# Memory read of a segmented attention as two row-half products, its last step on GpSimd, and vector steps with one operand in PSUM

## The chip, the cores and the metric

The kernel runs on one core of a Trainium2 chip. The metric is the device time of one execution in microseconds (us). The engines are TensorE (PE, with its weight loads PEld), VectorE (DVE), ScalarE (ACT), GpSimd (POOL) and SyncE (SP), whose queue issues most DMAs.

## The reference, cut to what matters

The output is `x + attention(xn) + mlp(xn)`, where `xn` is the layer-normalised input of 2048 tokens by 512. The attention has 32 heads of 16 and goes over 4 segments of 512 tokens. In each segment it mixes a causal softmax with a read of a memory that the earlier segments filled:

```python
for s in range(N):
    qs, ks, vs = q[:, :, s], k[:, :, s], v[:, :, s]
    logits = jnp.einsum("bhqd,bhkd->bhqk", qs, ks) * scale + mask
    p = _softmax(logits, axis=-1)
    a_dot = jnp.einsum("bhqk,bhkd->bhqd", p, vs)
    pq = phi(qs)                       # t + 1 where t > 0, exp(t) elsewhere
    num = jnp.einsum("bhld,bhde->bhle", pq, M)
    den = jnp.einsum("bhld,bhd->bhl", pq, z)[..., None] + 1e-6
    a_mem = num / den
    o = g * a_mem + (1.0 - g) * a_dot  # g = sigmoid(beta), one per head
    outs.append(o)
    pk = phi(ks)
    M = M + jnp.einsum("bhld,bhle->bhde", pk, vs)
    z = z + jnp.einsum("bhld->bhd", pk)
```

The MLP is a second layer norm, 512 to 1792 with GELU, and back to 512. All is float32.

## The kernel before, in words

The work is cut into 16 units: 4 segments times 4 groups of 8 heads (`i = 4 * s + g`). For a unit, queries and keys stand with 8 heads x 16 = 128 rows on the partitions and the segment's 512 tokens as columns. Beside the units runs the MLP in 16 half jobs (`d_job` for the first product, `gelu`, `h_split` for splitting the result in two f16 parts, `e` steps for the second product). Float32 products are made of f16 halves where the weights allow (`split3`: three products for one).

The steps of a unit, by the names that the profile's lines belong to:

- `qk_proj` (L599): projection of queries or keys, 12 matmuls of 512 columns at L586, then on ScalarE the high f16 half (L614) and, where `phi` is wanted, the exponential (L618). `qk_low` (L624) makes the low half on VectorE and sends both to DRAM over the SP queue; `qk_rows` (L646) loads them back in another layout, with 48 rows for each of two row halves.
- `qk_phi` (L632, L634, L638): two VectorE instructions, the first from SBUF to SBUF.
- `m_job` (L740, L747): products of 48 rows in the two row halves of the array, whose row maxima VectorE takes. `m_row` (L753 to L758) and `max_rows` (L763) carry the maxima through DRAM into two more rows of the queries' operand.
- `s_job` (L782, L789): the logits again, now with the maxima subtracted, and their exponentials on ScalarE; `s_mask` (L803) on GpSimd; `pv` (L816) the product with the values in four column tiles, in f32; `o_norm` the division: part 0 a shuffle, part 1 logarithm and exponential on ScalarE (L657, L658), part 2 a newton step on VectorE (L662, L663), part 3 on GpSimd the multiplication (L847) and the addition of the memory read (L849), parts 4 and 5 the split in halves.
- the memory: `pk_nat` (L651) turns the keys, `kv` (L717) adds to the memory `mst` and `zst`. For segments 1 to 3, `z_cols` (L670, L673) spreads `mst` and `zst` over the heads on VectorE, `a_mem` (L681 to L689) makes the read with the tokens as rows (4 products with 136 columns in f32, then six VectorE instructions with a reciprocal), and `a_turn` (L696, L698) turns it back with 4 transposes and a copy by ScalarE into `ame`.
- `out_jobs` (L951, L953): the output projection of a segment, added to the accumulator that `store` sends out.

The weights are loaded, scaled by a power of two (`w_scale`, L414) that comes from a sum of squares (`w_trace`, L382 and L384) and split in halves in the first 60 to 100 us, among the first units' work.

The schedule is written out by hand. `streams()` lists chains of steps, each with its name, a letter. The string `ORDER` says from which chain the next step is taken, and every engine's queue gets its instructions in that order. `BANKS` says for every product in turn which of PSUM's eight banks it takes; `dense()` draws the next digit. `plan()` also sets where ScalarE's tables are changed.

Of the kernel before, what the change touches and what calls it, by code (L numbers as in the profile page):

```python
# [9 lines left out]
F32 = mybir.dt.float32  # L10
# [9 lines left out]
P = 128  # L20
# [39 lines left out]
def streams():  # L60
# [78 lines left out]
    "auhhwhhhlkhhkhhbth6xc6khldlhhie$hfhhhhkjhx6f78$hhahhv$rg7%%8%k8%h8bR8cs8mRde8i&ff9m9gj9n&!n&#y&z((CA)9*(CD+(+2"  # L139
    "BBDo)(X*+X,)-,*(()X!*3oXX,9,XXYFZFF0Py1F.zpF,-o!FR4F#.Z-0FB9,.14BR4QFZF041/XZA,X/01/-/.4F$=4/=p:4E4P24#F2;F:=="  # L140
    "44:4G4GFGX=GF<XHGFF3>4HaI>::IHI>IFGqGb3Xc?X2GH;GFyFFdzG@XHf>XF:EHYCX<X?DiQZ0IIA>;IB1I>GJG<3KGXCLBe:XGG;ZHD@MPX"
    "4HNFFIIHQIO0IFFG1Z4f4<GGX?0@41GHHqFZFy0FGY>F4a[1?4zXjAFHFZIIIIb4@0B4414Z[[FEcJ4KXXd4440[1eBXfGGGZ4LXXFMG440G]F"
    "1FH4fUN4ZP^H0X1YFFFyH4OFFIIIZiAIGzF044444GFGCF]GGX4_ETX1H]H4Q]HIIIDIGJGKBGZH4LPVX0BaXy1ZzG0GFMC4X1H4AZ4^FID0H_"
    "NOIITIFG4XGFUG4H4G1GFHBH4XFFIIIIFFJYFKURR4B4FLFMbFZNFRXOE0S4W4GcFGeX4144HGGGRF5HFIIHQIIdFFGSZG5FHFPyG0GGXzSFH1"
    "Z2VHASIIQIEI0GJGKLGXC13BX2DPfUXTGMGW444fNZV44H0HHjIIIOQIBFFG41a4bGGX4iHGGF3Y44H4HFFF4yFZ5FI01IIzBZAI0F1JZFX04X"
    "C4K1DZ404FjXX1B44X4EXX4YT4Z44LFG2cG4M44eGFiFd01X43H4FGGZN0HXXFF5IHIIOIGFGXXGGF2XWFG1FZfHf0XPVHFU4441Z01YZyE44H"
    "a3zIIIQIGGJ44UK4L4C4AGGMTG4D4N4WH4bPHHOIIIIGGGXB0BVXGGFyFF1HzHHBFIcIdAIZIRCFFFe01RDXFJKFFXZi0RLMXXFWTN41fR4fE4"
    "GZGGB4440XHOG1FGH4SHFFFIIYIQISGGa5FVZ4X4GG0UFXP4HH2FG1Z0FbyH4FzFIQIIAI1S5XSPBFZJ4X03KLCc1EZDM4GiGT5NOG4XBXGGj4"
    "H4W0HH4IQIII1GGF444FGG4VXGFFyHHHFFFIYIII24dZ4e440F13zFZ0FJ4XC4D1Z0XXFEfXK41BTABXL4Z4XM44041GGGPX44UGFFH44HNU4f"
    "4OFYZGF04WXV44XH1F2ZFIIIIFGFy53G0zFFXX1XGHZGG44FHC440TXXXIED1QYI2HZI0IGG41JKH4BZjj44GGGH34L4UBMX4HWNXX0OIIIIFF"  # L150
# [902 lines left out]
```

## Time and profile before

| | |
|---|---|
| median of 3 runs | 691.14 us (690.75 to 691.84) |
| span of the profiled execution, first to last instruction | 690.7 us |
| PE busy | 680.1 us, 98% |
| PEld busy | 394.6 us, 57% |
| DVE busy | 498.9 us, 72% |
| ACT busy | 471.4 us, 68% |
| POOL busy | 346.4 us, 50% |
| DMA | 55.83 MB, mean 81 GB/s |

The profiled execution's own time is its span; the timed runs are other executions of the same program, and their median lies 0.4 us above it. A matmul's length in the profile holds the time until its last column has left the array, so that neighbours overlap: what a matmul costs is the distance from its start to the next one's. A group row reads: line, engine, operation, output and inputs, shapes, count, then busy time and mean length in ns, then the idle time of the engine ahead of it and what ended it. A row of the timeline begins with start and length in us. A row for one line alone gives the least, median and greatest length in ns and the first and last start. A row by stretches gives the stretch and, for each engine, its busy time in it.

### The profile page before, as it was taken

Reading aid. Unit: us, or ns where it says so; the run is one execution under the profiler, and the core shown is the slowest. Engines: PE = TensorE matmul, PEld = TensorE weight load, DVE = VectorE, ACT = ScalarE, POOL = GpSimd, SP = SyncE. Lnnn points to the kernel's source line nnn. Section 1 sums busy time; section 2 is a strip of 40 time slices with the busy share of each in tenths; the row PEclk is TensorE's granted clock in tenths of the full one; section 3 lists DMA queues with packets and bytes.
Section 4 is the critical chain, followed back from the end, with each engine's and each line's share of the span. In section 5 each row is a group of like instructions: output and inputs, shape, how many; then the busy total and the mean of one; then the engine's idle time right before and its main releaser. Section 6 shows DMA issues by size and latency. Waiting matters only on the chain.

```text
span 690.7 us, 15732 instructions
## 1 busy us (share of the span) xinstructions
PE 680.1 (98%) x5787; PEld 394.6 (57%) x5787; DVE 498.9 (72%) x1613; ACT 471.4 (68%) x877; POOL 346.4 (50%) x574
## 2 busy tenths in 40 slices
PE   8999999999999999999999999999999999999997
PEld 6764565656644565665555555566565446565543
DVE  5789888986796669676695875878468565787622
ACT  4578898897765578578836838556956554777960
POOL 5576587663525444373545344534372425365652
PEclk9999999999999999999999999999999999999999
DMA  9788433203320342312222133231411222420101
GB/s 267 230 199 218 113 91 105 79 2 91 81 49 16 87 108 55 95 47 72 70 70 57 31 79 86 57 85 39 99 35 56 69 65 61 107 65 2 33 1 61
DMA packets 52889, 55.83 MB, mean 81 GB/s; under 512 B 4990, under 2 KB 41868, under 8 KB 52812
## 3 DMA queue, kind: packets, MB, share of 16 engines
q1 hardware_dynamic: 50508, 50.64, 26.8%
q0 software_dynamic: 2304, 4.20, 3.8%
q8 instruction: 45, 0.74, 0.5%
q14 instruction: 32, 0.26, 0.1%
HBM read 37.77 MB, written 17.05 MB: 79 GB/s over the span
## 4 chain that ended last, share of the span: by engine, by line
PE 87%; DVE 8%; DMA 2%; issue 1%; SPq 1%; POOL 1%; ACT 0%; DVEq 0%
PE dense L586 35%; PE dense L931 20%; PE dense L816 10%; PE dense L951 6%; PE dense L782 6%; PE dense L740 5%; DVE dense L747 4%; PE dense L681 2%; PE dense L696 1%; DVE mc L747 1%; PE dense L564 1%; DMA pt<-in_A_wv_dram 1%; PE dense L651 1%; DMA qst<-md 1%; PE dense L382 0%
## 5 line engine op out<-in xcount | busy, mean ns | idle before, releaser
L747 DVE CUSTOM_DVE_ANT_0 dense<-dense,mask 128x384 f32<-128x384 f32 (+3 forms) x512 | 234.0, 528 | 33.9 <-PE dense L740 33.6
L789 ACT ACTIVATE pt<-dense,qkcs 128x512 f32<-128x512 f32 (+1 forms) x384 | 204.2, 628 | 46.3 <-PE dense L782 46.2
L931 PE MATMUL dense<-w2s,hT 128*128 128x512 f16 x672 | 166.3, 380 | 0.2 <-DVE hT L884 0.2
L586 PE MATMUL dense<-xnT,w1s 128*128 128x256 f16 x1344 | 160.2, 273 | 0.3 <-DVE mc L747 0.3
L803 POOL TENSOR_SCALAR_AFFINE_SELECT pt<-pt 128x256 f32<-128x256 f32 x256 | 99.4, 422 | 108.2 <-ACT pt L789 107.8
L586 PEld LDWEIGHTS <-w1s 128*128 128x128 f16 x1344 | 129.6, 98 | 29.1 <-issue 6.2
L905 POOL TENSOR_TENSOR hT<-hh,hT 128x512 f16<-128x512 f32 x64 | 67.6, 1057 | 83.6 <-ACT hT L903 70.4
L931 PEld LDWEIGHTS <-hT 128*128 128x128 f16 x672 | 61.3, 98 | 68.6 <-issue 13.4
L816 PE MATMUL dense<-pt,vt 128*32 128x512 f32 (+3 forms) x1024 | 78.0, 436 | 0.0
L747 DVE DVE_READ_ACCUMULATOR2_ANT mc<- 128x1 f32 x512 | 74.2, 145 | 0.0
L884 DVE SCALAR_TENSOR_TENSOR hT<-dense,sc,cb 128x512 f32<-128x512 f32 x64 | 43.5, 680 | 33.8 <-PE dense L586 25.2
L847 POOL TENSOR_TENSOR nN<-nN,oT 128x512 f32<-128x512 f32 x16 | 20.9, 1308 | 73.9 <-DVE oT L663 73.9
L901 POOL TENSOR_SCALAR hh<-hT,sc 128x512 f32<-128x512 f32 x64 | 42.5, 664 | 24.1 <-ACT hT L891 15.5
L816 PEld LDWEIGHTS dense<-pt,vt 128*32 128x32 f32 x1024 | 31.1, 109 | 40.7 <-issue 29.4
L782 PE MATMUL dense<-qst,kst 50*128 50x384 f16 (+3 forms) x512 | 52.1, 299 | 1.8 <-DMA qst<-md 1.8
L740 PE MATMUL dense<-kst,qst 48*128 48x384 f16 (+3 forms) x512 | 52.2, 298 | 0.0
L891 ACT ACTIVATE hT<-hT,b1t 128x256 f32<-128x256 f32 x112 | 47.0, 496 | 5.0 <-DVE hT L884 4.6
L903 ACT ACTIVATE hT<-hh 128x512 f16<-128x512 f32 x64 | 37.3, 583 | 14.9 <-POOL hh L901 14.9
L951 PE MATMUL dense<-wos,oT 128*128 128x512 f16 (+2 forms) x204 | 44.0, 367 | 0.8 <-DVE acc L953 0.7
L586 PE MATMUL dense<-xnT,wks 128*128 128x512 f16 (+1 forms) x252 | 44.5, 329 | 0.2 <-DVE mc L747 0.2
L586 PE MATMUL dense<-xnT,wqs 128*128 128x512 f16 (+1 forms) x252 | 44.2, 329 | 0.1
L586 PE MATMUL dense<-wvs,xnT 128*128 128x512 f16 x192 | 43.9, 379 | 0.1
(227 smaller groups left out, 832.0 us busy)
## 6 DMA issues: line engine op xcount, KB each, us to landing
kst<-kd SPq DMA_DIRECT2D x32, 192.0 KB
qst<-qd SPq DMA_DIRECT2D x32, 192.0 KB
qd<-hl SPq DMA_DIRECT2D x36, 128.0 KB
kd<-hl SPq DMA_DIRECT2D x33, 128.0 KB
acc<-in_A_x_dram SPq DMA_DIRECT2D x16, 256.0 KB
acc<-in_B_b_dram POOLq DMA_DIRECT2D x16, 256.0 KB, 4.2
out_dram<-acc SPq DMA_DIRECT2D x15, 256.0 KB
xt<-in_A_x_dram SPq DMA_DIRECT2D x14, 256.0 KB
```

The costliest lines, as they stand in the source:

```text
L586: T.matmul(p, ws(k, a), xs(k, b), start=i == 0, stop=i == 3 * KT - 1)
L740: T.matmul(p[:, o:o + n], stk[i, 0][r, t, P * qb:P * qb + P], stk[i, 1][r, t, :n], start=True, stop=True)
L747: V.tensor_tensor_reduce(p[:, o:o + n], p[:, o:o + n], mask[:, 512 - n:], 1.0, -3e38, OP.add, OP.max, mc[i][:, 4 * b + t, qb:qb + 1])
L782: T.matmul(p[:, o:o + n], stk[i, 1][r, t, P * kb:P * kb + P], stk[i, 0][r, t, P * kb:], start=True, stop=True)
L789: A.activation(pt[i, 4 * b + t][:, OFF[kb]:OFF[kb] + n], p[:, c:c + n], AF.Exp, scale=qkcs[:, 1, i % NG:i % NG + 1])
L803: G.affine_select(v, v, pattern=[[0, 2], [1, P]], compare_op=OP.is_ge, fill=0.0, base=0, channel_multiplier=-1)
L816: T.matmul(p[32 * c:32 * c + 32, P * kb:], vt[s, kb][:, 4 * g + c, 16 * odd:16 * odd + 32], pt[i, 2 * c + odd][:, OFF[kb]:OFF[kb] + LEN[kb ...
L884: V.scalar_tensor_tensor(hz[:, f0:f + 1, :], p[:, :256 * n].rearrange("p (f c) -> p f c", f=n), col(CG + fh), cbt[hf].unsqueeze(1).to_broa ...
L891: A.activation(hz[:, f, :], hz[:, f, :], AF.Gelu_apprx_tanh, bias=b1t[:, fo:fo + 1])
L905: G.tensor_tensor(hT[:, z, 1, :], hht[j, c], hT[:, z, 0, :], op=OP.subtract)
L931: T.matmul(p, t[:, u, P * a:P * a + P], w2s[:, fo, v, :], start=fi == 0 and n == 0, stop=fi == FH - 1 and n == 2)
L951: T.matmul(p[:, c], o[:, u, P * b:P * b + P], wos[:, g, v, c], start=i == 0, stop=i == 3 * NG - 1)
```

## The change

- **phi.** `qk_proj` no longer makes the exponential. A new step `qk_floor` (`Tu`) has VectorE write `max(p * c, 0)` from PSUM into SBUF and ScalarE make the exponential from PSUM into the same PSUM bank. `qk_phi` is one VectorE instruction, `min(exp, 1) + floor`, with one operand in PSUM and one in SBUF.
- **memory read.** `z_cols` runs on GpSimd and writes 128 columns, which hold 64 of the memory with the gate's factor and 64 of the normaliser. `a_mem` has the tokens as columns: two f32 products, one with the upper and one with the lower 64 rows, each giving 64 rows of numerators and 64 of denominators by 512 columns. ScalarE takes the denominators' logarithm (two instructions of 64 rows) and one exponential of the negative. `a_share` (`Y`) has four VectorE instructions of 64 rows, each with one operand in PSUM. `a_step` (`Yg`) ends it with two GpSimd instructions. The turn by TensorE, its copy and the reciprocal are gone.
- **softmax division.** `o_norm` part 1 writes the exponential to a PSUM bank, and the newton step reads it there.
- **small things.** The addition to `zst` moves to GpSimd; `gates` and `qk_scale` have fewer small instructions.
- **order.** `ORDER` and `BANKS` are new as a whole: from the step `T` of unit 0 on, the steps stand in another order, the last steps too.

```diff
@@ streams @@
             put(n + "1", ("Tv", i, w))
             if not (s == 0, s == NSEG - 1)[w]:
+                put(n + "1", ("Tu", i, w))
                 put(n + "2", ("Tw", i, w))
...
-            put("mem2", ("Qt", i))
+            put("mem2", ("Y", i))
+            put("mem3", ("Yg", i))
@@ ORDER, BANKS: new strings @@
@@ qk_proj @@
-        e = None
-        if phi:
-            e = sb.tile([P, 512], F32, name=("phq", "phk")[which])
-            A.activation(e, p, AF.Exp, scale=qkcol(2, 1 - which, g))
-        prj[i, which] = p, hl, e
+        prj[i, which] = p, hl
...
+    def qk_floor(i, which):
+        g = i % NG
+        p = prj[i, which][0]
+        e = pqt[i, which] = sb.tile([P, 512], F32, name=("phq", "phk")[which])
+        c = qkcol(2, 1 - which, g)
+        V.tensor_scalar(e, p, c, 0.0, op0=OP.mult, op1=OP.max)
+        A.activation(p, p, AF.Exp, scale=c)
+
     def qk_phi(i, which):
...
-        V.tensor_scalar(e, e, 1.0, qkcol(3, 1 - which, g), op0=OP.min, op1=OP.mult)
         if which == 0:
-            V.scalar_tensor_tensor(e, p, 0.0, e, op0=OP.max, op1=OP.add)
+            V.scalar_tensor_tensor(e, p, 1.0, e, op0=OP.min, op1=OP.add)
@@ the memory read @@
     def z_cols(i):
-        g = i % NG
-        mx[i] = sm.tile([P, P + GH], F32, name="mx")
-        V.tensor_tensor(mx[i][:, :P] ...
-        V.tensor_scalar(mx[i][:, P:], half, zst[:, g:g + 1], None, op0=OP.mult)
+        s, g = divmod(i, NG)
+        if s == 1:
+            G.tensor_scalar(quadg[:, g], quad, bg[:, g, 3:4], 0.0, op0=OP.mult, op1=OP.add)
+        mx[i] = sm.tile([P, P], F32, name="mx")
+        G.tensor_tensor(mx[i][:, :64] ...
+        G.tensor_scalar(mx[i][:, 64:] ...
     def a_mem(i):
-        for t in range(4):
-            T.matmul(ps[t // 2][:, t % 2, :], pqt[i, 0][:, P * t:P * t + P], mx[i], start=True, stop=True)
-        (six VectorE instructions, L684 to L691)
-    def a_turn(i):
-        for t in range(4):
-            T.transpose(p[:, P * t:P * t + P], amt[i][:, P * t:P * t + P], ident)
-        ame[i] = sb.tile([P, 512], F32, name="ame")
-        A.activation(ame[i], p, AF.Copy)
+        q = pqt[i, 0]
+        mp[i] = [dense() for b in range(2)]
+        R = [slice(64 * b, 64 * b + 64) for b in range(2)]
+        for r, p in zip(R, mp[i]):
+            T.matmul(p, mx[i][r, :], q[r, :], start=True, stop=True)
+        for r, p in zip(R, mp[i]):
+            A.activation(q[r, :], p[64:, :], AF.Ln, bias=tiny[:64])
+        A.activation(q, q, AF.Exp, scale=-1.0)
+
+    def a_share(i):
+        q = pqt[i, 0]
+        t = ame[i] = sb.tile([P, 512], F32, name="ame", bufs=2)
+        R = [slice(64 * b, 64 * b + 64) for b in range(2)]
+        for r, p in zip(R, mp[i]):
+            V.tensor_tensor(t[r, :], p[:64, :], q[r, :], op=OP.mult)
+            V.scalar_tensor_tensor(q[r, :], p[64:, :], 1e-6, q[r, :], op0=OP.add, op1=OP.mult)
+
+    def a_step(i):
+        q, t = pqt[i, 0], ame[i]
+        G.tensor_scalar(q, q, -2.0, 0.0, op0=OP.add, op1=OP.add)
+        G.tensor_tensor(t, t, q, op=OP.mult)
@@ kv @@
-        V.tensor_tensor(zst[:, g:g + 1], zs[i], zst[:, g:g + 1], op=OP.add)
+        G.tensor_tensor(zst[:, g:g + 1], zs[i], zst[:, g:g + 1], op=OP.add)
@@ o_norm @@
         elif part == 1:
-            log_recip(nd[i][2], d)
+            rec[i] = dense()
+            A.activation(d, nd[i][2], AF.Ln)
+            A.activation(rec[i], d, AF.Exp, scale=-1.0)
         elif part == 2:
-            newton(nd[i][2], nd[i][2], d)
+            r = nd[i][2]
+            V.tensor_tensor(r, r, rec[i], op=OP.mult)
+            V.scalar_tensor_tensor(r, r, 2.0, rec[i], op0=OP.subtract, op1=OP.mult)
```

More of the change, by code (lines that the diff above doesn't have):

```diff
@@ L144 @@
[L144 to L148, printed above, removed]
@@ L399, in qk_scale @@
         h = h.unsqueeze(2).to_broadcast([P, 2, n])
-        f, s, c, t = (qksc[:, j, :, g0:g0 + n] for j in range(4))
+        f, s, c = (qksc[:, j, :, g0:g0 + n] for j in range(3))
         power(s, h, -1, 203)
```

121 lines of the change are left out of this document (52 added, 69 removed).

## The prediction

> **What bounds the kernel now.** I read the page first (engine shares, the chain that ended last), then the groups of instructions with shapes kept apart, then the timeline of TensorE where the changed products stand.
>
> ```profile
> span 690.7 us, 15732 instructions
> PE 680.1 (98%) x5787; PEld 394.6 (57%) x5787; DVE 498.9 (72%) x1613; ACT 471.4 (68%) x877; POOL 346.4 (50%) x574
> PEclk9999999999999999999999999999999999999999
> PE 87%; DVE 8%; DMA 2%; issue 1%; SPq 1%; POOL 1%; ACT 0%; DVEq 0%
> ```
>
> TensorE is busy for 98% of the span at full clock, and 87% of the chain that ended last is its work; no other engine is over 72%. The sum is therefore one of TensorE's time, plus the few places where it waits. The two stretches in which another engine is nearest to the bound are seen in a view by stretches (PE, PEld, DVE, ACT, POOL):
>
> ```profile
> 75.00:160.00 85.00, 84.75 (x789) 50.30 (x788) 73.98 (x243) 75.54 (x141) 57.63 (x96) 1.00 0.26 66
> 160.00:660.00 500.00, 499.57 (x4276) 285.58 (x4274) 357.85 (x1152) 336.39 (x625) 233.01 (x390) 1.00 0.25 64
> ```
>
> From 160 to 660 us, where all twelve memory reads lie, TensorE is idle for 0.4 us of 500, with VectorE at 72%, ScalarE at 67% and GpSimd at 47%. From 75 to 160 us ScalarE is at 89% and VectorE at 87%: there is the place that bears least.
>
> **TensorE's part, step by step.** The memory read and its surroundings (start, length, engine, line; a length holds the drain of the last matmul, so I go from start to start):
>
> ```profile
> 208.75 1.67 PE L951 MATMUL dense<-wos,oT 128*128 128x512 f16 x7
> 210.26 0.81 PE L931 MATMUL dense<-w2s,hT 128*128 128x512 f16 x3
> 210.91 0.60 PE L696 MATMUL dense<-ident,rc 128*128 128x128 f32 x4
> 211.35 0.81 PE L931 MATMUL dense<-w2s,hT 128*128 128x512 f16 x3
> 212.09 0.39 PE L782 MATMUL dense<-qst,kst 50*128 50x512 f16 x2
> 212.32 0.38 PE L740 MATMUL dense<-kst,qst 48*128 48x384 f16 x4
> ...
> 651.23 1.09 PE L681 MATMUL dense<-mx,phq 128*128 128x136 f32 x8
> 652.25 0.65 PE L782 MATMUL dense<-qst,kst 50*128 50x512 f16 x6
> 652.83 0.82 PE L931 MATMUL dense<-w2s,hT 128*128 128x512 f16 x3
> 653.59 0.47 PE L782 MATMUL dense<-qst,kst 50*128 50x256 f16 x4
> 653.99 2.76 PE L931 MATMUL dense<-w2s,hT 128*128 128x512 f16 x12
> 656.68 2.36 PE L816 MATMUL dense<-pt,vt 128*32 128x512 f32 x32
> 658.97 0.82 PE L782 MATMUL dense<-qst,kst 50*128 50x512 f16 x8
> ```
>
> 1. A full 512-column f16 matmul takes (210.26 - 208.75)/7 = 0.216 us.
> 2. A change between full array and row halves costs 0.10 us: three matmuls of L931 from 652.83 end at 653.48, the next starts at 653.59. From L931 to the transposes there is none (210.26 + 0.65 = 210.91).
> 3. Gone per unit: the four turns at L696, 211.35 - 210.91 = 0.44 us, and the eight records of L681, 652.25 - 651.23 less one change = 0.92 us. Twelve units: 12 x 1.36 = **-16.3 us**.
> 4. Added per unit: two f32 products of 64 rows by 512 columns. L816's 32 records are four f32 column tiles at a time over 512 + 384 + 256 + 128 = 1280 columns: 658.97 - 656.68 - 0.10 = 2.19 us, so an f32 pass over 512 columns takes 0.88 us. Whether two row halves in f32 run at the same time no row shows. Bounds: 0.88 us if they do, 1.76 if they don't. The nearest row says they do: the two row halves of L782 at 212.09 (512 columns each, f16) take 0.23 us until 212.32, the price of one. I take 0.88: 12 x 0.88 = **+10.6 us**, with +21.1 as the other end.
> 5. The new order. Walking both order strings through the stream table, and marking each step by what it uses (row halves: `m_job`, `s_job` and the new `a_mem`; column tiles: `pv`, `kv`; all else the full array), gives 266 changes of tiling before and 291 after; of the new products nine of twelve follow a step of `m_job` or `s_job` and nine are followed by one, so they cost few changes themselves. 25 x 0.10 = **+2.5 us**. All other TensorE steps are the same in number.
>
> Steady sum: -16.3 + 10.6 + 2.5 = -3.2 us.
>
> **The waits at the start**, the only ones of any size on TensorE:
>
> ```profile
> 33.14 1.47 PE L586 MATMUL dense<-xnT,w1s 128*128 128x256 f16 x12
> 35.61 0.38 PE L414 MATMUL dense<-am,ones 128*128 128x1 f32 x2 [1.00 <-DVE dense L384]
> L632 DVE TENSOR_SCALAR phk<-phk,qksc x12: 450/558/1384, 30.6 to 452.2; 128x512 f32<-128x512 f32 x12
> 30.58 1.38 DVE L632 TENSOR_SCALAR phk<-phk,qksc 128x512 f32<-128x512 f32 x1
> L782 PE MATMUL dense<-qst,kst 50*128 50x512 f16 x128 | 25.1, 382 | 1.8 <-DMA qst<-md 1.8
> 62.72 2.63 DMA md<-mhl
> 65.67 3.85 DMA qst<-md
> ```
>
> The first is `w_scale("2a")` behind a `d_job`, which waits for VectorE's sum at L384. In the new order the transposes of `pk_nat(0)` (four like those at L696, 0.44 us) stand ahead of it on TensorE, and VectorE's queue in front of L384 loses the 1.38 us instruction, whose successor reads PSUM at some 0.7 us. 0.44 + 0.7 covers the whole wait: -0.9 (bounds -1.0 and 0). The second is the round trip of unit 0's maxima (`m_row` to the first `s_job`). Between the two TensorE had seven `e` steps, one `pk_nat` and two `m_job`; now it has one `d_job` more (12 matmuls like those at 33.14: 1.47 less the drain, 1.3 us). On the SP queue unit 1's `qk_rows` with two 192 KB loads now stands between the two small transfers, which may delay the second. Bounds -1.3 and +1; I take -0.7.
>
> **The other engines, costed and laid beside TensorE.**
>
> ```profile
> L684 DVE TENSOR_SCALAR rd<-dense,qkcs 128x16 f32<-128x16 f32 x24 | 4.8, 228 | 4.5 <-PE dense L681 4.5
> L685 DVE RECIPROCAL rd<-rd 128x32 f32<-128x32 f32 x12 | 4.2, 353 | 0.4
> L686 DVE SCALAR_TENSOR_TENSOR rd<-rd,qkcs,gr 128x32 f32<-128x32 f32 x12 | 3.9, 322 | 0.4
> L689 DVE TENSOR_TENSOR rc<-dense,rd 128x256 f32<-128x256 f32 x24 | 9.1, 419 | 0.4
> L670 DVE TENSOR_TENSOR mx<-mst,half 128x128 f32<-128x128 f32 x12 | 4.1, 339 | 0.0
> L673 DVE TENSOR_SCALAR mx<-half,zst 128x8 f32<-128x8 f32 x12 | 2.9, 238 | 0.0
> L634 DVE SCALAR_TENSOR_TENSOR phq<-dense,phq x12: 691/692/692, 163.8 to 606.0; 128x512 f32<-128x512 f32 x12
> L632 DVE TENSOR_SCALAR phq<-phq,qksc 128x512 f32<-128x512 f32 x12 | 7.3, 612 | 1.9 <-ACT phq L618 1.9
> L698 ACT ACTIVATE ame<-dense 128x512 f32<-128x512 f32 x12 | 7.5, 622 | 11.6 <-POOL nN L849 7.6 <-PE dense L696 3.9
> L658 ACT ACTIVATE nD<-nD 128x512 f32<-128x512 f32 x16 | 10.1, 630 | 0.5
> L849 POOL TENSOR_TENSOR nN<-nN,ame 128x512 f32<-128x512 f32 x12 | 15.3, 1273 | 0.9
> L901 POOL TENSOR_SCALAR hh<-hT,sc 128x512 f32<-128x512 f32 x48 | 34.7, 724 | 23.1 <-ACT hT L891 15.5 <-issue 5.7
> 653.63 0.76 DVE L689 TENSOR_TENSOR rc<-dense,rd 128x256 f32<-128x256 f32 x2
> ```
>
> VectorE loses 4.8 + 4.2 + 3.9 + 9.1 + 4.1 + 2.9 = 29.0 us and gains 48 instructions of `a_share` at 0.69 (L634, a PSUM and an SBUF operand) = 33.2. The 24 instructions of L632 become one that reads PSUM: between 0.45 (the least of L632) and 0.69; against the queries' mean of 0.61 that is 24 x 0.08 = +1.9, since a part of the old ones is held up. VectorE ends some 6 us higher, near 505 us.
>
> The Trainium skill, "VectorE: DVE Perf Modes", section Why PSUM operands drop a tier, speaks against this step: an operand in PSUM shuts out the mode in which an f32 instruction with one input runs at two elements per cycle. The least of L632 agrees; by the rule alone VectorE would pay 24 x 0.24 = 5.8 us for the move, by the measured mean 1.9. Neither is on TensorE's path, so the forecast is the same by both.
>
> ScalarE loses L698 (7.5) and gains per unit two logarithms and one exponential at 0.63 (L658): 12 x 1.89 = 22.7, so +15 us to about 486, or 71% of the new span. GpSimd gains 12 x (0.72 + 1.27) = 23.9 for `a_step` and 24 small instructions of `z_cols` that I put at 0.35 each, between nothing and L901's 0.72: +32, to about 380 us, 55%. I cost all this at nothing: TensorE's stream covers it, as the stretch from 160 to 660 us shows for loads of 67 to 72%. If that cover goes, a memory read costs what follows its product: two logarithms, an exponential, four VectorE steps and two of GpSimd, 1.9 + 2.8 + 2.0 = 6.7 us. Behind the new waits stand, on ScalarE, the exponentials of `s_job`; on VectorE, the maxima of `m_job`; on GpSimd, the masks of `s_mask` that `pv` needs, and the two multiplications of `o_norm`. The last unit's `a_step` stands in front of `o_norm` part 3 on GpSimd, in a gap that this row shows:
>
> ```profile
> 673.37 1.27 POOL L847 TENSOR_TENSOR nN<-nN,oT 128x512 f32<-128x512 f32 x1 [2.84 <-DVE oT L663]
> ```
>
> 2.84 us of idle time take the 2.0 us, so the end is not moved. The newton steps with one operand in PSUM (`o_norm` part 2) cost the same 0.69. The removed rows of `qk_scale` and `gates` are instructions of 0.1 to 0.4 us, off TensorE's path.
>
> **Sum.** Against the span: 690.7 - 3.2 - 0.9 - 0.7 = 685.9. The runs' median, 691.14, stands 0.4 above the span: **686.3 us**.
>
> **Rivals.**
> - The row halves do not overlap in f32 (place: each of twelve products). Price +10.6 over my sum: 696.9, slower. It decides from 1.3 us per pair upward, where the twelve give back 5 us. For it: no row shows f32 in row halves, and an f32 product goes through the array more than once. Against it: f16 row halves overlap at L782, f32 column tiles at L816. 7%.
> - The gain goes into new waits on PSUM's eight banks or on ScalarE. A memory read held two banks from 651.23 to VectorE's last read at 653.63 + 0.76 (3.2 us); now they are held through 0.88 + 1.9 + 2.8 = 5.6 us, and `o_norm` takes a bank more for 2.0 us. In the stretch from 75 to 160 us ScalarE has 9.5 us of slack. A wait of 0.3 us per memory read plus 1 us in the loading phase gives 690.9: no change. Against it: 0.4 us of idle time in 500. 16%.
> - The waits shrink further: VectorE's instructions are no longer held up by GpSimd's, the other short waits of TensorE for VectorE go, and the order at the start is better filled. Some 3 us: 683. 10%.
>
> The Trainium skill, "SBUF — State Buffer", section Who interferes with whom, says that an instruction of VectorE with two SBUF inputs, or in the mode with two ports, contends with GpSimd and that one with a single SBUF input does not; L632's 450 to 1384 ns fit that. By the rule the third rival gains weight, but the waits it could lift are off TensorE's path.
>
> **How the numbers follow.** Forecast 67%, the three rivals 7, 16 and 10%. A difference of 0.2% (1.4 us) is about what can be told from no change. The forecast with its bounds (waits at the start from -2.3 to +1, changes of tiling) runs from 684.5 to 689; third rival down to 682, second up to 691.5; first left out. Range 681.5 to 691.5. Faster: 67 + 10 + 3 of the second; same: 11; slower: 7 + 2.
>
> **What would show it.** Records of the new product in pairs a few ns apart, about 0.88 us from the first to the next line's first; no turn at the old L696; TensorE's group sums down by some 6 us for the memory read. `w_scale("2a")` without its wait of 1.00; the idle time ahead of `s_job` under 1.8. VectorE near 505, ScalarE 486, GpSimd 380 us. `qk_floor`'s VectorE instruction at 0.69 with little spread. The prediction is wrong if the halves run one after the other (1.76 us a pair), or if TensorE shows idle time released by ScalarE or VectorE in the stretch to 160 us or behind the new products.

## The result and the profile after

The changed kernel takes 696.63 us (median, 695.84 to 696.98) against 690.94 us (689.53 to 691.84) for the kernel before on the same chip: 1.0083 times as long, interval 1.0069 to 1.0098. The forecast was 686.3 us.

The page of the changed kernel, the rows that answer to those of before (span, engines, chain by engine):

```profile
span 695.3 us, 15559 instructions
PE 682.0 (98%) x5691; PEld 382.0 (55%) x5691; DVE 506.2 (73%) x1552; ACT 490.6 (71%) x900; POOL 392.6 (56%) x635
PE 67%; ACT 12%; POOL 7%; DVE 7%; DMA 3%; issue 2%; SPq 1%; POOLq 0%; ACTq 0%; DVEq 0%
```

Line numbers are those of the changed kernel: L588 is the f16 product of the projections and of the MLP, L735 and L742 are `m_job`'s products and maxima, L777 is `s_job`, L798 the masks, L811 `pv`, L883 the instruction that scales the MLP's first product (`hT`) and so frees its PSUM bank, L687 and L688 are `a_share`, L692 and L693 `a_step`. In the other runs they differ by a few lines.

The shares of the engines hardly differ, and PE is still at 98%. What moved is the chain that ended last: TensorE's part falls from 87% to 67%; ScalarE and GpSimd, which had 0 and 1%, have 12 and 7%. The kernel is no longer held by TensorE alone. The same two stretches as before (us, then PE, PEld, DVE, ACT and POOL):

```profile
75.00:160.00 85.00, 84.86 (x772) 49.38 (x773) 73.20 (x240) 76.20 (x144) 59.62 (x102) 1.00 0.28 70
160.00:660.00 500.00, 495.76 (x4135) 271.47 (x4127) 362.38 (x1094) 351.00 (x641) 269.85 (x436) 1.00 0.25 63
```

From 75 to 160 us, which the prediction took for the place that bears least, TensorE is as busy as before (84.86 us for 84.75). From 160 to 660 us TensorE is idle for 4.2 us instead of 0.4. What it waits for there (line of TensorE, what it waited for, total, times, longest):

```profile
PE dense L777 <- DMA qst<-md: 0.9, 1, 0.9
PE dense L588 <- DVE mc L742: 0.8, 1, 0.8
PE dense L811 <- POOL pt L798: 0.6, 1, 0.6
PE dense L735 <- DMA out_dram<-acc: 0.4, 1, 0.4
PE dense L811 <- DVE phq L688: 0.4, 1, 0.4
PE dense L777 <- ACT nD L820: 0.4, 1, 0.4
PE dense L735 <- DVE hT L883: 0.3, 1, 0.3
```

The records hide part of the waits: a record's length holds the drain (0.38 us for a full f16 matmul whose successor can start 0.22 us after it), so a start that is late by less than the difference leaves no idle time. So I also added up TensorE from start to start over all records: what its columns take at the best rate seen, 0.097 us for each change of tiling, and the rest, which is waiting. In us, for the profiled execution of each kernel:

| kernel | columns | changes | waits | of these behind 160 us |
|---|---|---|---|---|
| before | 630.2 | 25.8 | 17.9 | 6.1 |
| after | 624.1 | 28.2 | 26.5 | 14.9 |

Columns fall by 6.1, changes rise by 2.4, waits rise by 8.6: 4.9 us more, against 4.6 by the spans. On TensorE's columns the new memory read does what it says. The loss is waits: 8.8 us more behind 160 us, where all twelve memory reads lie, and 0.2 us less ahead of it (11.6 for 11.8).

One line stands out there, `a_step`'s first instruction (least, median and greatest length in ns):

```profile
L692 POOL TENSOR_SCALAR phq<-phq x12: 1923/1938/2243, 182.7 to 675.2; 128x512 f32<-128x512 f32 x12
```

Beside it, among the groups of the changed kernel, its second instruction and the one whose price the prediction took for the first (L901 there; busy us, mean ns):

```profile
L900 POOL TENSOR_SCALAR hh<-hT,sc 128x512 f32<-128x512 f32 x48 | 33.4, 695 | 40.9 <-ACT hT L890 29.2 <-issue 9.7 <-DMA qst<-qd 0.2
...
L693 POOL TENSOR_TENSOR ame<-ame,phq 128x512 f32<-128x512 f32 x12 | 15.3, 1271 | 1.0
```

All three work on 128 x 512 in f32; L692 takes 1.94 us where 0.72 was put. And it stands in the chain of waits ahead of TensorE's longest new stop, 0.6 us in the list above and 1.7 us from start to start (the chain in order of time; start, length, what):

```profile
396.62 1.91 POOL phq L692
...
398.60 1.27 POOL ame L693
399.87 0.25 POOL mx L665
400.12 0.30 POOL mx L669
400.43 1.45 POOL pt L798 x4
401.88 1.13 POOL hT L904
...
403.81 1.10 POOL pt L798 x3
404.91 0.04 issue
404.95 1.20 PE dense L811 x13
```

Read upwards: `pv` (L811) starts its last part when the masks of L798 are there; GpSimd came to these only after both instructions of `a_step` and the two of `z_cols` (L665, L669). There is a second way in which `a_step` holds others. It has the one buffer `phq` until it ends, and the next unit's `qk_floor` on VectorE needs it:

```profile
610.80 0.75 DVE L631 TENSOR_SCALAR phq<-dense,qksc 128x512 f32<-128x512 f32 x1 [2.00 <-POOL ame L693]
```

VectorE stands still for 2.00 us, with the maxima of `m_job` queued behind, and TensorE waits 0.8 us for them (L588 <- DVE mc L742 above).

### The profile page after: what moved, and what is told of

Same layout as the page of the kernel before. It is cut to its first block, busy times and chain, and to the rows that moved or that the text cites. A ratio compares the mean times of both kernels' runs of the same rounds, so it can differ in the third digit from the quotient of the medians.

```text
span 695.3 us, 15559 instructions
## 1 busy us (share of the span) xinstructions
PE 682.0 (98%) x5691; PEld 382.0 (55%) x5691; DVE 506.2 (73%) x1552; ACT 490.6 (71%) x900; POOL 392.6 (56%) x635
## 4 chain that ended last, share of the span: by engine, by line
PE 67%; ACT 12%; POOL 7%; DVE 7%; DMA 3%; issue 2%; SPq 1%; POOLq 0%; ACTq 0%; DVEq 0%
PE dense L588 28%; PE dense L930 14%; PE dense L811 8%; PE dense L950 5%; PE dense L735 5%; ACT pt L784 5%; PE dense L777 4%; POOL phq L692 1%; ACT hT L890 1%; POOL pt L798 1%; DVE dense L742 1%; PE dense L677 1%; POOL hT L904 1%; POOL ame L693 1%; ACT phq L679 1%
## 5 line engine op out<-in xcount | busy, mean ns | idle before, releaser
L742 DVE CUSTOM_DVE_ANT_0 dense<-dense,mask 128x384 f32<-128x384 f32 (+3 forms) x512 | 234.8, 524 | 34.5 <-PE dense L735 33.4
L588 PE MATMUL dense<-xnT,w1s 128*128 128x256 f16 x1344 | 161.3, 273 | 1.8 <-DVE mc L742 0.8
L798 POOL TENSOR_SCALAR_AFFINE_SELECT pt<-pt 128x256 f32<-128x256 f32 x256 | 99.5, 416 | 103.2 <-ACT pt L784 102.8
L588 PEld LDWEIGHTS <-w1s 128*128 128x128 f16 x1344 | 129.2, 98 | 33.3 <-issue 8.7
L811 PE MATMUL dense<-pt,vt 128*32 128x512 f32 (+3 forms) x1024 | 80.6, 436 | 1.2 <-POOL pt L798 0.6
L742 DVE DVE_READ_ACCUMULATOR2_ANT mc<- 128x1 f32 x512 | 72.2, 141 | 0.1
L883 DVE SCALAR_TENSOR_TENSOR hT<-dense,sc,cb 128x512 f32<-128x512 f32 x64 | 43.5, 680 | 34.3 <-PE dense L588 33.5
L811 PEld LDWEIGHTS dense<-pt,vt 128*32 128x32 f32 x1024 | 32.7, 109 | 45.1 <-issue 27.6
L777 PE MATMUL dense<-qst,kst 50*128 50x512 f16 (+3 forms) x512 | 55.3, 298 | 1.5 <-DMA qst<-md 0.9
L735 PE MATMUL dense<-kst,qst 48*128 48x384 f16 (+3 forms) x512 | 54.9, 298 | 0.9 <-DMA out_dram<-acc 0.4
L588 PE MATMUL dense<-xnT,wks 128*128 128x512 f16 (+1 forms) x252 | 44.5, 329 | 0.1
L588 PE MATMUL dense<-xnT,wqs 128*128 128x512 f16 (+1 forms) x252 | 44.2, 328 | 0.0
L588 PE MATMUL dense<-wvs,xnT 128*128 128x512 f16 x192 | 43.4, 379 | 0.0
L735 PEld LDWEIGHTS <-qst 48*128 48x128 f16 x512 | 20.6, 94 | 33.3 <-issue 24.9
```

Of the source, the lines that this page charges most:

```text
L588: T.matmul(p, ws(k, a), xs(k, b), start=i == 0, stop=i == 3 * KT - 1)
L735: T.matmul(p[:, o:o + n], stk[i, 0][r, t, P * qb:P * qb + P], stk[i, 1][r, t, :n], start=True, stop=True)
L742: V.tensor_tensor_reduce(p[:, o:o + n], p[:, o:o + n], mask[:, 512 - n:], 1.0, -3e38, OP.add, OP.max, mc[i][:, 4 * b + t, qb:qb + 1])
L777: T.matmul(p[:, o:o + n], stk[i, 1][r, t, P * kb:P * kb + P], stk[i, 0][r, t, P * kb:], start=True, stop=True)
L798: G.affine_select(v, v, pattern=[[0, 2], [1, P]], compare_op=OP.is_ge, fill=0.0, base=0, channel_multiplier=-1)
L811: T.matmul(p[32 * c:32 * c + 32, P * kb:], vt[s, kb][:, 4 * g + c, 16 * odd:16 * odd + 32], pt[i, 2 * c + odd][:, OFF[kb]:OFF[kb] + LEN[kb ...
```

## The experiments

### The slow instruction

Theory A: the form of the first instruction, two additions on GpSimd, is slow, and all that stands behind it on GpSimd pays. The rivals: the banks, the order, VectorE's operands.

`step_mult`, the same value by another form:

```diff
-        G.tensor_scalar(q, q, -2.0, 0.0, op0=OP.add, op1=OP.add)
+        G.tensor_scalar(q, q, 1.0, -2.0, op0=OP.mult, op1=OP.add)
```

> The first instruction of a_step, on GpSimd, written as q * 1 + (-2) in place of (q + (-2)) + 0: the same numbers, another pair of operations, nothing else. In the changed kernel it took 1.94 us twelve times where I had put 0.72. Theory A (the slow form is what takes the gain: it stands ahead of masks, of the multiplications of o_norm and of the next unit's qk_floor): the instruction falls to about 0.70 us, GpSimd's busy time by 14 to 15 us to 378, the three largest waits (1.9 us at 402, 1.3 us at 571, 1.0 us at 612) shrink by 1.2 us each or go, and the time falls by 4 to 6 us to 691 or 692. Theory B (the new order and the longer-held PSUM banks make the waits, the form only shows up as the last one in line): the instruction falls as well but the time by less than 1.5 us, to 695 to 696.6.

`step_twice`, the slow form two times, adding -1 each:

```diff
-        G.tensor_scalar(q, q, -2.0, 0.0, op0=OP.add, op1=OP.add)
+        G.tensor_scalar(q, q, -1.0, 0.0, op0=OP.add, op1=OP.add)
+        G.tensor_scalar(q, q, -1.0, 0.0, op0=OP.add, op1=OP.add)
```

> The slow instruction twice (each adds -1), so that the sum is the same and GpSimd has 12 x 1.94 = 23 us more. Theory A: the waits grow by at least as much as they shrink in the other direction per us, 23 us more against 15 us less: the time rises by 6 to 12 us, to 703 to 708. Theory B: GpSimd has slack at 56% busy, the time rises by less than 2 us.

`step_vector`, the whole step as one VectorE instruction with both operands in SBUF:

```diff
-        G.tensor_scalar(q, q, -2.0, 0.0, op0=OP.add, op1=OP.add)
-        G.tensor_tensor(t, t, q, op=OP.mult)
+        V.scalar_tensor_tensor(t, q, -2.0, t, op0=OP.add, op1=OP.mult)
```

> a_step as one VectorE instruction, (q + (-2)) * t with both operands in SBUF, in place of the two on GpSimd; same order and banks. GpSimd loses 12 x 3.2 = 38 us, VectorE gains 12 x 0.7 = 8.5 us. Theory A: all waits behind a_step on GpSimd go, 690 to 692, no worse than the multiplied form although it has two operands in SBUF. Theory B: 695 to 697. A third reading (the operands in SBUF are what matters: such an instruction is held up by GpSimd and holds it up): its median is well over 0.7 us, some over 1.5, and the time stays above that of the multiplied form by 1 us or more.

`step_none`, with `a_step` left out:

```diff
-        G.tensor_scalar(q, q, -2.0, 0.0, op0=OP.add, op1=OP.add)
-        G.tensor_tensor(t, t, q, op=OP.mult)
```

> a_step left out altogether (the reciprocal's correction is missing from the memory read), same order and banks: the bound for everything that the last step on GpSimd costs. Theory A: 689 to 691, that is most of the distance to the sum of TensorE's work. Theory B: 694 to 696.

| kernel | median us | ratio to before (interval) | POOL busy | TensorE's waits |
|---|---|---|---|---|
| after | 696.63 | 1.0083 (1.0069 to 1.0098) | 392.6 | 26.5 |
| step_mult | 693.18 | 1.0043 (1.0025 to 1.0061) | 377.1 | 23.2 |
| step_twice | 708.85 | 1.0265 (1.0247 to 1.0282) | 415.6 | 35.6 |
| step_vector | 693.60 | 1.0042 (1.0030 to 1.0054) | 357.3 | 22.4 |
| step_none | 691.42 | 1.0013 (0.9996 to 1.0031) | 354.8 | 20.6 |

The instruction in `step_mult` and in `step_vector`:

```profile
L692 POOL TENSOR_SCALAR phq<-phq x12: 620/622/910, 182.1 to 671.8; 128x512 f32<-128x512 f32 x12
```

```profile
L692 DVE SCALAR_TENSOR_TENSOR ame<-phq,ame x12: 669/685/1620, 181.8 to 674.0; 128x512 f32<-128x512 f32 x12
```

That the form is slow, and that it costs time, is shown in both directions. The same number of elements, the same type and engine: 0.62 us as multiply and add, 1.94 us as two additions. Twelve times 1.32 us off GpSimd gave back 3.4 us of time by the medians (2.8 by the ratios), twelve times 1.94 us more cost 12.2 us; per us of GpSimd's time that is 0.2 and 0.5. Gaps that are used up first would explain the difference; that is argued, not shown. In `step_twice` TensorE's waits name the same places, 3.4 us for the masks of `pv` and 2.8 us for the maxima. The three waits of TensorE that the expectation of `step_mult` names, at 402, 571 and 612 us, are gone in that run: from start to start no more than 0.45 us is left at any of them. In size theory A missed all four times: 693.18 where it had 691 to 692, 708.85 for 703 to 708, 693.60 for 690 to 692, 691.42 for 689 to 691. The third reading of `step_vector` fell too: with both operands in SBUF the median is 0.685 us, and the time is 0.4 us above `step_mult`, not 1. And `step_none` shows that the last step is not all: with no last step whatever the kernel is where the kernel before is, not 4.8 us under it.

### What is left: banks, operands or VectorE

Each of the next three puts one part of the change back, on top of `step_mult`. `mult_rec_sbuf`, `o_norm`'s exponential back in SBUF:

```diff
-            rec[i] = dense()
+            next(banks)
             A.activation(d, nd[i][2], AF.Ln)
-            A.activation(rec[i], d, AF.Exp, scale=-1.0)
+            A.activation(d, d, AF.Exp, scale=-1.0)
...
-            V.tensor_tensor(r, r, rec[i], op=OP.mult)
+            V.tensor_tensor(r, r, d, op=OP.mult)
```

> The changed kernel with the fast form of a_step's first instruction (as in step_mult, 693.2 us, ratio 1.0043), and beside it o_norm's exponential written to SBUF as in the kernel before, so that no PSUM bank is held for it (the bank is drawn and left empty) and the two Newton instructions of VectorE have two SBUF operands again. Theory B (part of what step_mult still loses is PSUM banks held longer, here by o_norm for some 2 us per unit): TensorE's waits shrink, 691.5 us or less. Theory O (what is left is the order itself: 25 more tiling changes, 2.4 us, and waits of its own for maxima and for data coming back by DMA): no difference from step_mult within 0.7 us, 692.5 to 693.9. Theory S (contention between VectorE instructions with two SBUF operands and GpSimd is what the change saved): slower than step_mult by 1 us or more.

`mult_z_vector`, `z_cols` back on VectorE:

```diff
-        G.tensor_tensor(mx[i][:, :64].rearrange(...
+        V.tensor_tensor(mx[i][:, :64].rearrange(...
-        G.tensor_scalar(mx[i][:, 64:].rearrange(...
+        V.tensor_scalar(mx[i][:, 64:].rearrange(...
```

> The changed kernel with the fast form of a_step's first instruction, and beside it z_cols (24 small instructions, 8.5 us in step_mult) back on VectorE. GpSimd falls from 377 to some 369 us, VectorE rises from 506 to some 513. Theory G (GpSimd's queue still sets waits in step_mult): 1 us or more faster than step_mult, 692 or less. Theory O (the order): within 0.7 us of step_mult, 692.5 to 693.9. Theory V (VectorE's queue is next: m_job's maxima stand behind the added instructions): slower by 1 us or more, 694.2 and up.

`mult_phi_sbuf`, phi as before:

```diff
-        V.tensor_scalar(e, p, c, 0.0, op0=OP.mult, op1=OP.max)
-        A.activation(p, p, AF.Exp, scale=c)
+        A.activation(e, p, AF.Exp, scale=c)
...
+        V.tensor_scalar(e, e, 1.0, qkcol(3, 1 - which, g), op0=OP.min, op1=OP.mult)
-            V.scalar_tensor_tensor(e, p, 1.0, e, op0=OP.min, op1=OP.add)
+            V.scalar_tensor_tensor(e, p, 0.0, e, op0=OP.max, op1=OP.add)
```

> The changed kernel with the fast form of a_step's first instruction, and beside it phi as in the kernel before: the exponential goes to SBUF, VectorE takes its min and factor there (0.45 to 0.61 us each instead of 0.74 from PSUM), and the last instruction reads projection and exponential as before. VectorE falls by 24 x 0.15 = 3.6 us to some 502. Theory V (VectorE's queue sets the waits that are left): 0.5 to 1.5 us faster than step_mult, 691.7 to 692.7. Theory S (with one operand in SBUF VectorE no longer holds up GpSimd and is no longer held up): slower than step_mult by 1 us or more. Theory O: within 0.7 us, 692.5 to 693.9.

| kernel | median us | ratio to before (interval) | DVE busy | TensorE's waits |
|---|---|---|---|---|
| step_mult | 693.18 | 1.0043 (1.0025 to 1.0061) | 505.8 | 23.2 |
| mult_rec_sbuf | 693.11 | 1.0041 (1.0025 to 1.0056) | 507.6 | 22.5 |
| mult_z_vector | 695.96 | 1.0081 (1.0064 to 1.0098) | 509.5 | 24.9 |
| mult_phi_sbuf | 694.15 | 1.0046 (1.0029 to 1.0063) | 504.1 | 23.1 |

Two parts of the change, the exponential in PSUM and phi from PSUM, make no difference that these runs can tell, for the better or the worse; the gain of 0.5 to 1.5 us that theory V had for `mult_phi_sbuf` did not come. So the bank that `o_norm` keeps is not what costs, and it is not fewer VectorE operands in SBUF that saves. `z_cols` is another matter: 3.7 us more on VectorE cost 2.6 to 2.8 us. One new wait stands out (the longest wait of TensorE in `mult_z_vector` from 160 us):

```profile
PE dense L677 <- DVE phq L638: 1.9, 1, 1.9
```

The memory read's product (L677) waits for phi, whose instructions stand behind the ones of `z_cols` in VectorE's queue. But what made these late is a wait of their own:

```profile
252.31 0.39 DVE L665 TENSOR_TENSOR mx<-mst,quadg 128x64 f32<-128x64 f32 x1 [5.35 <-POOL quadg L663]
```

`z_cols` reads `quadg`, which the edit left on GpSimd, and VectorE stood still for 5.35 us until it was there. So the run shows that `z_cols` costs time on VectorE as it is put there, with a wait for GpSimd in front of phi; that VectorE at 73% could not take the 3.7 us themselves is not shown. Nor is the 1.9 us the whole account: TensorE's waits grew by 1.7 us in all, 0.9 us of it in a wait for a load at the start (L384 <- DMA wvs, 1.8 us against 0.9).

### The old order

`old_order_mult` has the new operations, with the fast form, in the order of the kernel before; `before_rebank` is the kernel before with the banks given out by the rule that the former needed (new strings only).

> The changed kernel's operations with the fast form of a_step's first instruction, merged into the order of the kernel before: the removed transposes left out, a_share four steps behind a_mem, a_step ten behind that, phi's floor instruction in front of phi's last one; banks given out anew by a simple rule. 277 tiling changes instead of 291 (and 266 before). Theory O (the new order costs what step_mult still loses): TensorE pays 690.9 - 6.1 (streaming) + 1.1 (11 more changes) = 686 us where this order causes no waits of its own, and anything under 691 supports it. Theory M (the memory read's new operations cost waits in any order, since two 64-row products, three ScalarE and four VectorE instructions follow one another): 692 us or more, with TensorE's waits behind the memory reads and not in the loading phase. before_rebank in the same call says what the other banks cost by themselves.

> The kernel before, its operations and its order, with the PSUM banks given out by the same simple rule as in old_order_mult. A control: if it is within 1.4 us of the kernel before (689.5 to 692.3), the rule for the banks costs nothing and old_order_mult can be read for its order and operations alone; if it is slower, that much of old_order_mult's time is the banks.

They took 732.22 us (1.0609, 1.0591 to 1.0627) and 703.02 us (1.0194, 1.0168 to 1.0220). The control failed: the simple rule for the banks costs 12.4 us in the kernel before itself; its profiled execution has 26.4 us of waits on TensorE instead of 17.9. What the rule costs with the new operations no run shows, so the pair says nothing sure about the order. Whether the new order by itself costs waits stays open; its 25 more changes of tiling, at 0.097 us each, are 2.4 us.

### VectorE behind the memory read

`no_newton` drops the Newton step of the memory read, so that the read has the precision of one logarithm and one exponential; the gate's factor changes its sign:

```diff
             V.tensor_tensor(t[r, :], p[:64, :], q[r, :], op=OP.mult)
-            V.scalar_tensor_tensor(q[r, :], p[64:, :], 1e-6, q[r, :], op0=OP.add, op1=OP.mult)
...
-        G.tensor_scalar(q, q, -2.0, 0.0, op0=OP.add, op1=OP.add)
-        G.tensor_tensor(t, t, q, op=OP.mult)
...
-        V.tensor_scalar(bg[:, :, 3], bg[:, :, 0], -1.0, None, op0=OP.mult)
+        V.tensor_scalar(bg[:, :, 3], bg[:, :, 0], 1.0, None, op0=OP.mult)
```

> The changed kernel's memory read without its Newton step: the second instruction of each half in a_share (24 on VectorE, 692 ns each, 16.6 us) and both of a_step on GpSimd are left out, and the gate's factor is +1 instead of -1, so that the read is num times exp(-ln den) directly. It tells apart what is left over the kernel before in step_none (691.4 us, which keeps all of a_share and leaves out a_step only). Theory V (what is left are waits on VectorE: a_share is four instructions in a row, 2.9 us, in front of maxima and hT in its queue, and z_cols back on VectorE cost 2.8 us in mult_z_vector): VectorE falls to some 489 us, TensorE's waits at 262, 346 and 433 us go, 689.5 us or less. Theory O (what is left are tiling changes and waits for DMA and the order's own): within 0.7 us of step_none, 690.7 to 692.1.

`no_newton_fix` moves one letter of `ORDER`, the accumulating load of token block 14, behind unit 14's first `s_job`.

> As no_newton, and one step of the order moved: the accumulating load of 256 KB for token block 14 (A, GpSimd's queue, issued at 613.2 us in step_mult) goes behind unit 14's first s_job. In step_mult the maxima's small store, issued at 614.2, took 4.9 us beside that load and another of the same kind, and TensorE waited 1.1 us for them to come back. Theory D (the load is what slows the small store): the store takes some 1 to 2 us less, the wait of about 1.1 us at 619 falls to 0.3 or goes, and the time is 0.7 to 1.1 us under no_newton. Otherwise (the store is late for VectorE's sake, or the first of the two loads alone slows it): the wait stays, no difference.

`no_newton` took 689.02 us, 0.9976 (0.9966 to 0.9986), and `no_newton_fix` 688.73 us, 0.9973 (0.9962 to 0.9985). Both are faster than the kernel before, without the Newton step. Against `step_none`, which lacks the same GpSimd work, leaving out 24 instructions of VectorE (16.6 us) gave 2.4 us. What they stood in front of is seen on VectorE's timeline, in `step_mult`:

```profile
429.99 0.68 DVE L687 TENSOR_TENSOR ame<-dense,phq 64x512 f32<-64x512 f32 x1 [0.84 <-ACT phq L680]
430.71 0.69 DVE L688 SCALAR_TENSOR_TENSOR phq<-dense,phq 64x512 f32<-64x512 f32 x1
431.43 0.69 DVE L687 TENSOR_TENSOR ame<-dense,phq 64x512 f32<-64x512 f32 x1
432.15 0.69 DVE L688 SCALAR_TENSOR_TENSOR phq<-dense,phq 64x512 f32<-64x512 f32 x1
432.88 0.48 DVE L883 SCALAR_TENSOR_TENSOR hT<-dense,sc,cb 128x256 f32<-128x256 f32 x1
```

and in `no_newton`:

```profile
426.96 1.40 DVE L687 TENSOR_TENSOR ame<-dense,phq 64x512 f32<-64x512 f32 x2 [0.84 <-ACT phq L680]
428.39 0.48 DVE L881 SCALAR_TENSOR_TENSOR hT<-dense,sc,cb 128x256 f32<-128x256 f32 x1
```

In both, `a_share` starts when ScalarE's exponential is ready, 0.84 us after VectorE ran out of work; `hT`, whose bank TensorE needs, comes 2.9 us later in the first and 1.4 us later in the second. TensorE's waits from 160 to 660 us, first of `step_mult`, then all of `no_newton`:

```profile
PE dense L777 <- DMA qst<-md: 1.1, 1, 1.1
PE dense L735 <- DVE mc L742: 0.7, 1, 0.7
PE dense L811 <- DVE phq L688: 0.4, 1, 0.4
PE dense L735 <- DMA out_dram<-acc: 0.3, 1, 0.3
PE dense L735 <- DVE hT L883: 0.3, 1, 0.3
```

```profile
PE dense L733 <- DMA out_dram<-acc: 0.4, 1, 0.4
```

The waits for `phq`, `hT` and the maxima `mc` are gone, and so is the one for the maxima on their way through DRAM (`qst<-md`). The moved load did what it was meant to, in a small way. The maxima's store (L751 or L753) and the load behind it, in `step_mult` and in `no_newton_fix`:

```profile
613.23 1.20 POOL L912 DMA_DIRECT2D acc<-in_B_b_dram  x1
614.21 0.30 SPq L753 DMA_DIRECT2D md<-mhl  x1
619.13 0.53 SPq L758 DMA_DIRECT2D qst<-md  x2
```

```profile
611.01 0.30 SPq L751 DMA_DIRECT2D md<-mhl  x1
613.83 0.53 SPq L756 DMA_DIRECT2D qst<-md  x2
```

From the store to the load that waits for it are 4.92 us in `step_mult`, beside two accumulating loads of 256 KB. The run to compare with is `no_newton`, which has both loads as well: 3.75 us there, 2.82 us with one of them moved away. In `no_newton` the wait was 0.28 us already (of TensorE's weight load), so that the gain of 0.7 to 1.1 us that was expected could not come, and the timed runs show no difference (0.3 us between the medians).

### Total load, or the place?

`no_newton_load` and `no_newton_load2` put the 24 instructions back on VectorE, but into `o_norm`, where they do nothing; the first reads PSUM, the second SBUF alone. `mult_split` parts `a_share` in two blocks of two instructions, on top of `step_mult`.

```diff
             V.scalar_tensor_tensor(r, r, 2.0, rec[i], op0=OP.subtract, op1=OP.mult)
+            for _ in range(2 if s else 0):
+                V.scalar_tensor_tensor(r, rec[i], 0.0, r, op0=OP.mult, op1=OP.add)   # no_newton_load
+                V.tensor_tensor(r, r, r, op=OP.max)                                  # no_newton_load2, in its place
```

```diff
+        if later and (later[1] == 0 or key[0] == "Yg"):    # three steps behind "Y"
+            a_share(later[0], 1)                           # the second half
+            later.clear()
         CALL[key[0]](*key[1:])
```

> As no_newton, and 24 instructions of VectorE with one operand in PSUM (r = 0 * rec + r, 128 x 512, some 0.69 us each) added in o_norm part 2, two in each unit from 4 to 15: VectorE carries the same 506 us as in step_none, but not in the memory read. Theory T (VectorE's total load sets the waits that no_newton was rid of): back at step_none's time, 691.4 us within 0.7. Theory B (it is the place: four instructions in a row in front of the maxima, hT and the PSUM banks in VectorE's queue, behind each memory read): the load is hidden where o_norm stands, 689.0 to 689.7 us. In between: both.

> The changed kernel with the fast form of a_step's first instruction (step_mult, 693.2 us, ratio 1.0043), and a_share's second half three steps of the order later than its first, so that two instructions stand in a row on VectorE instead of four; the same instructions in all. Theory B (the block of four in VectorE's queue): the waits of TensorE at 262 (1.1 us), 346 (0.5 us) and 433 us (0.7 us) shrink by half or more, 691.5 to 692.4 us. Theory T (total load): no difference, 692.5 to 693.9. Slower than that: the second half's PSUM bank, held some 1 to 2 us longer, is what the next steps wait for.

> As no_newton_load (699.3 us), with the 24 added instructions of VectorE reading SBUF alone (r = max(r, r), 128 x 512), at the same place in o_norm part 2: the PSUM bank of o_norm's exponential is free before them, 1.4 us earlier. no_newton_load's chain of waits showed TensorE's s_job waiting for exactly that bank (0.9 us at 457, 1.0 at 586), but also VectorE's hT behind it. Theory P (what costs is the bank: VectorE's instruction stands between TensorE and a bank it needs): 689 to 692.5 us. Theory Q (what costs is the place in VectorE's queue, whatever the operands: hT, maxima and the memory read stand behind): 697 us or more. In between: shares of both. Theory T (total load alone: as step_none): 691.4 us within 0.7.

| kernel | median us | ratio to before (interval) | DVE busy | TensorE's waits |
|---|---|---|---|---|
| no_newton | 689.02 | 0.9976 (0.9966 to 0.9986) | 489.8 | 18.1 |
| step_none | 691.42 | 1.0013 (0.9996 to 1.0031) | 505.8 | 20.6 |
| no_newton_load | 699.26 | 1.0119 (1.0106 to 1.0132) | 505.4 | 27.2 |
| no_newton_load2 | 699.71 | 1.0136 (1.0119 to 1.0152) | 506.0 | 26.9 |
| mult_split | 694.57 | 1.0055 (1.0042 to 1.0067) | 506.5 | 23.5 |

Both of my theories for `no_newton_load` fell: I had expected nothing or 2.4 us, and 10.2 us came. With VectorE at 505 to 506 us in each, the price of the same 16.6 us is 2.4 us behind the memory read and 10 us in `o_norm`. So its total load is not what decides. Nor is the bank: without it the time is the same, and the wait only changes its name. Near 459 us TensorE stopped for `o_norm`'s bank (0.9 us, L775 <- DVE oT L844) and then 0.3 us for `hT` in the first, and in the second for `hT` alone:

```profile
455.86 0.69 DVE L841 TENSOR_TENSOR oT<-oT,dense 128x512 f32<-128x512 f32 x1 [1.18 <-ACT dense L838]
456.59 0.69 DVE L842 SCALAR_TENSOR_TENSOR oT<-oT,dense 128x512 f32<-128x512 f32 x1
457.31 1.42 DVE L844 TENSOR_TENSOR oT<-oT 128x512 f32<-128x512 f32 x2
458.64 0.75 DVE L883 SCALAR_TENSOR_TENSOR hT<-dense,sc,cb 128x512 f32<-128x512 f32 x1
```

```profile
459.44 1.25 PE L588 MATMUL dense<-xnT,w1s 128*128 128x256 f16 x10 [1.54 <-DVE hT L883]
```

What decides is what stands behind an instruction in its queue: 1.42 us of added work and 1.18 us of idle time ahead of it make TensorE wait 1.54 us. VectorE stood still right before, so that its idle time could not take the work: it lies on the wrong side of a wait. The Trainium skill, "Perfetto Trace Analysis", section Optimizing Scalar/DVE Operations, says that breaking up instructions may let work be done sooner where ScalarE or VectorE isn't saturated but causes bubbles on other engines. `mult_split` comes near that, though it parts a block of four instructions and not an instruction, and it brought no gain here (1.0055 against 1.0043).

The longer hold of the second PSUM bank, the last of the readings recorded for it, is what the traces of `mult_split` point to. The wait for the maxima that ended at 263.3 us in `step_mult` (0.7 us) is gone; in its place TensorE waits until 262.0 us for the second half of `a_share`, which reads that bank (L694 here, L688 in `step_mult`):

```profile
PE dense L741 <- DVE phq L694: 1.8, 2, 1.3
```

With 0.9 and 0.4 us of two other products, TensorE's waits for this half are 3.1 us from 160 to 660 us, against 0.4 us in `step_mult`.

## Why the prediction was wrong, point by point

**TensorE's steps 3 to 5 held.** The products' halves overlap: four records a read, and the next line's first start 0.92 us later in the mean of the twelve, changes of tiling included, 0.86 us where none borders on them (the prediction had 0.88). All records of L677:

```profile
L677 PE MATMUL dense<-phq,mx x48: 587/590/693, 167.7 to 658.3; 64*128 64x512 f32 x48
```

Columns fell by 6.1 us (forecast 16.3 - 10.6 = 5.7) and changes of tiling cost 2.4 (forecast 2.5). The rival of halves one after the other, whose 696.9 us is by chance the time that came, is refuted by this row.

**The waits at the start: one of two went.** The maxima's round trip of unit 0 lost its wait, as forecast (1.8 us to nothing in that line, 0.2 us for another load instead). `w_scale("2a")` kept 0.4 of its 1.0 us, but the steps drawn ahead of it wait themselves:

```profile
34.74 1.26 PE L588 MATMUL dense<-xnT,w1s 128*128 128x256 f16 x10 [0.78 <-POOL w1s L454]
...
36.81 0.38 PE L414 MATMUL dense<-am,ones 128*128 128x1 f32 x2 [0.37 <-DVE dense L386]
```

The forecast asked whether work stood ahead of the wait, not whether that work's own operand, a split of the weights on GpSimd, was ready. The -0.9 came out at 0.78 + 0.37 - 1.00 = +0.15. Over all waits ahead of 160 us the -1.6 came out at -0.2.

**The step that failed** is "I cost all this at nothing: TensorE's stream covers it, as the stretch from 160 to 660 us shows for loads of 67 to 72%". That nothing came out at 8.8 us, the rise of the waits behind 160 us: of the miss it is by far the largest part. The step has two faults.

The first is a size: "GpSimd gains 12 x (0.72 + 1.27)" took the first instruction from L901, a multiplication and an addition of the same shape and type. The instruction costed has two additions and takes 1.94 us. With 0.62 us in its place (`step_mult`) the time falls by 3.4 us (2.8 by the ratios), so that much of the miss of 10.3 us is this size. The Trainium skill, "GPSIMD Engine Reference", section 4.1 Engine selection, calls GpSimd's instructions with one input "roughly line-rate". The 0.62 us, beside 0.69 us for VectorE's instruction of this shape in `step_vector`, agrees with that; the 1.94 us does not.

The second is the reasoning: an engine's share of busy time was read as cover. VectorE came out at 506.2 us (forecast 505), ScalarE at 490.6 (486), near what was summed, GpSimd at 392.6 (380) for the size above, and no engine but TensorE over 73%. Still 24 instructions of VectorE (16.6 us) cost 2.4 us, what was left of `a_step` 1.8 us (by the medians; the two intervals overlap), and the same 16.6 us at another place 10 us. The prediction had listed what stands behind the memory read on each engine (the masks, the maxima, the exponentials), and the masks and the maxima are what TensorE then waited for. But no price was worked out from the list; the 16% for new waits, with 690.9 us, was the right kind of rival with too small a size; it looked to PSUM's banks, ScalarE and the loading phase, while the waits came from GpSimd's and VectorE's queues behind 160 us.

**The account.** `no_newton` should be 3.5 us under the kernel before by the table's terms (-6.1 + 2.4 + 0.2), and the timed runs have 1.6. The table compares one execution of each kernel, and the one of the kernel before was long: its span is 690.7 us, and the medians of that kernel's spans beside the later runs are 688.6 to 689.3 us. So its waits are some 1.4 to 2.1 us above the usual. The rest is a difference between time and span: 1.6 to 1.8 us in the kernel before, 2.0 to 2.1 us in `no_newton`. The 0.4 us that the prediction added for it compares two different executions.

**What stays open.** The 2.4 us of changes of tiling were in the forecast and are no part of the miss. `no_newton`, which lacks the Newton step, is 1.6 us under the kernel before; the forecast had 4.8 us with that step. Its waits behind 160 us are 7.2 us, against 6.1 us in the long execution of the kernel before. Where the other 3 us went, and whether an order of its own, made for the fast form, would bring the full 4.8 us, was not settled.

## What to carry to other kernels

Price every new instruction by a row with the same operation pair, not only the same shape, engine and type; where no row has the pair, bound it by the slowest row of that engine. An engine at 73% covers new work only where the work does not stand between a wait and what a fuller engine needs next: for each instruction added, find the next instruction in its queue that the bound engine waits for, and how much slack that one had. Where one slow instruction is suspected, take it away and double it; the two together show both its price and whether the price is linear.

## What the runs showed of the hardware that was not expected

- GpSimd, 128 x 512 f32 to f32, one input: 0.62 us as multiply and add, 1.94 us as add and add.
- Two f32 products in two row halves, 512 columns each, overlap: 0.86 us for both, 0.92 us in the mean with the changes of tiling beside them.
- From the issue of a store of 16 KB to that of the load that waits for it: 4.92 us with two accumulating loads of 256 KB issued 1.0 and 2.1 us earlier (`step_mult`), 3.75 us with two issued 2.3 and 3.4 us earlier (`no_newton`), 2.82 us with one issued 3.4 us earlier (`no_newton_fix`), 1.81 us in the kernel before, where none was issued in the 20 us ahead of it.
